# Attention over a long key cache on one core: K loaded in 8 KB rows and 1 MB transfers, V in 1 MB transfers, pairs of groups two apart

## The chip, the cores and the metric

The kernel runs on one core of one Trainium2 chip. The metric is the device time of one execution in microseconds (us), as the median of several runs. The profile of an execution has a span that is about 1.8 us shorter than that time. In the profile's lines PE is TensorE, DVE is VectorE, ACT is ScalarE, POOL is GpSimd and SP is SyncE. A DMA moves its bytes in packets; it has landed when its last semaphore update has come. A load here gives 16 such updates, as many as the profile counts DMA engines; below, each landing is read as that of one engine.

## The reference, cut to what matters

```python
B, Hq, Hkv, Sq, Sk, D = 16, 32, 8, 16, 2048, 128        # bf16 inputs
def reference(q, k, v):
    k = jnp.repeat(k, 4, axis=1); v = jnp.repeat(v, 4, axis=1)
    scores = jnp.einsum("bhqd,bhkd->bhqk", q, k) * D ** -0.5
    return jnp.einsum("bhqk,bhkd->bhqd", softmax(scores), v)
```

There are 16 x 8 = 128 groups. One group is one K and one V matrix of 2048 x 128 (512 KB each) and the 64 query rows (4 heads x 16) that share it. K and V are 134 MB together and every byte is used once. Q and the output are 2.1 MB each.

## The kernel before: the parts that the change and the argument touch

Two adjacent groups form a pair, so that 2 x 64 query rows fill 128 partitions. Each pair takes these steps: load K and V, transpose K on VectorE (one `eng.transpose` of 128 x 1024 32-bit words for each group, 1.24 us; the score matmuls then read it 32 partitions at a time), scores on TensorE, exp on ScalarE, transpose P on TensorE, copy it out of PSUM, P times V, scale by 1/rowsum, store. The order of instructions on each engine is fixed when the kernel is built, by a list scheduler in the kernel file. All DMAs are issued by SyncE, in one fixed order.

```python
# transfers, all on SP
if kind == "K":      # one group, 512 KB: 128 partitions x 4 KB
    dst, src = Kn[s].bitcast(BF16), kf[x].rearrange("(a j) d -> a (j d)", j=16)
elif kind == "V":    # one group, 512 KB: 128 partitions x 4 KB
    dst, src = Vb[s], vf[x].rearrange("(a j) d -> a j d", j=16)
...
else:                # ST: one pair, 32 KB: 128 partitions x 256 B
    dst, src = of[128 * x:128 * (x + 1), :], Osb[s]
sp.dma_start(dst, src).then_inc(prog.sem_dma[kind][s], 16)
...
# K transposed, then scores and exp over the 2048 keys of a pair
eng.transpose(KT[(p // 2) % NKT][:, p % 2, :], Kn[p % NBK])
eng.activation(P[p % 2]..., S_ps..., ACT.Exp, scale=scale, accum_out=rowsum[:, p:p+1])
...
# the end: exp without a maximum is safe only for sums within a range; if not, all is done again
eng.wait_ge(sem_flag, 4)
eng.reg_load(reg, flag)
eng.br_eq(reg, all_within, on_true=after, on_false=redo).branch_hint(hints[me])
```

Every engine ends with a branch over a large block of code (the second program, for the unsafe case). A hint for that branch (`branch_hint`) is placed some operations before the end (`HINT = {"pe": 7, "dve": 10, "act": 3, "pool": 1, "sp": 6}`).

## Time and profile before

| | before |
|---|---|
| time, median (runs) | 357.49 us (357.17 to 357.58) at first; 355.4 to 357.9 over all later runs |
| span of the profiled execution | 353.4 us |
| busiest compute engine | DVE, 68% of the span |
| packets of the kernel's DMA queue | 98.7% of 16 engines' span |

These lines of the profile's page of the kernel before give the span, the DMA share and rate in 40 slices of the span, the packets, the queues, and the kernel's DMAs with the median time from issue to landing.

```profile
span 353.4 us, 11937 instructions
...
DMA  7999999999999999999999999999999999999971
GB/s 276 414 408 408 413 408 407 412 413 406 413 408 410 412 410 412 408 413 411 410 411 411 408 412 413 395 411 413 409 411 409 406 413 410 403 409 405 411 287 42
DMA packets 47288, 139.24 MB, mean 394 GB/s; under 512 B 13440, under 2 KB 13440, under 8 KB 47232
...
q1 hardware_dynamic: 47232, 138.43, 98.7%
q8 instruction: 43, 0.70, 0.8%
...
Kn<-in_k_dram SPq DMA_DIRECT2D x128, 512.0 KB, 12.1
Vb<-in_v_dram SPq DMA_DIRECT2D x128, 512.0 KB, 13.3
...
out_dram<-O SPq DMA_DIRECT2D x64, 32.0 KB, 11.0
```

The reader should see a kernel that is bound by its DMA engines from slice 2 on: the DMA row stays at 9 up to slice 38, and no compute engine is busy for more than 68% of the span. By these figures only fewer bytes, cheaper packets or fewer packets can help inside the stream.

The trace's packet records give the price of a packet. The median is 159 ns for 4096 B, 84 ns for 2048 B, 18 ns for 256 B and 9 ns for a semaphore write of 4 B. A fit to these four is about 150 ns per 4 KB plus 9 ns per packet.

The second place to look is the end. These lines are the branch and the DRAIN that follows it on each engine (on SP, waits for the stores come between them, from 352.87 us on), from the queries for source lines 372 and 379; the columns are durations in ns and the start in us.

```profile
L372 ACTq COMPARE_BRANCH  x1: 72/72/72, 349.2 to 349.2; - x1
...
L372 SPq COMPARE_BRANCH  x1: 70/70/70, 349.6 to 349.6; - x1
...
L379 POOLq DRAIN  x1: 123/123/123, 349.7 to 349.7; - x1
L379 PEldq DRAIN  x1: 62/62/62, 349.8 to 349.8; - x1
L379 ACTq DRAIN  x1: 80/80/80, 352.6 to 352.6; - x1
L379 DVEq DRAIN  x1: 58/58/58, 352.7 to 352.7; - x1
L379 SPq DRAIN  x1: 7/7/7, 353.2 to 353.2; - x1
```

POOL and PE go on 0.5 us after the branch. ACT, DVE and SP stand still for 3.3 us, although the last store had landed at 350.10 us (the trace's semaphore landings). The chain of waits ends with the last scaling, at 348.28 + 0.35 = 348.63 us:

```profile
347.16 1.10 PE O_ps L355 x32
348.26 0.03 issue
348.28 0.35 DVE O L290
```

### The profile page before, as it was taken

The numbers are of one execution on the slowest core, as the hardware profiler recorded it, in microseconds if no ns is written. First come the engines' busy times: TensorE is split into PE (matmuls) and PEld (weight loads), VectorE is DVE, ScalarE is ACT, GpSimd is POOL, SyncE is SP. The second block draws the span as 40 slices with busy tenths as digits, with TensorE's granted clock in tenths as the row PEclk, the third lists the DMA queues.
The fourth block names the chain that finished last, engine by engine and source line by source line (L and its number), as shares of the span: only waits on it lengthen the run. The fifth ranks groups of instructions, "written<-read, shape, count | busy, mean of one in ns | idle before, by whom it ended". The sixth has DMA issues, their size and how long they took to land.

```text
span 353.4 us, 11937 instructions
## 1 busy us (share of the span) xinstructions
PE 233.8 (66%) x5378; PEld 167.9 (48%) x5378; DVE 239.4 (68%) x340; ACT 193.8 (55%) x214; POOL 28.9 (8%) x35
## 2 busy tenths in 40 slices
PE   2499765776666857756556876676656677566663
PEld 1266543554444634544444655454444545444442
DVE  4668786787685666766766676675776647866761
ACT  6458555754347646665456753576554755554450
POOL 1040000300012000310004000040000400000000
PEclk9999999989999998999999988999999989999997
DMA  7999999999999999999999999999999999999971
GB/s 276 414 408 408 413 408 407 412 413 406 413 408 410 412 410 412 408 413 411 410 411 411 408 412 413 395 411 413 409 411 409 406 413 410 403 409 405 411 287 42
DMA packets 47288, 139.24 MB, mean 394 GB/s; under 512 B 13440, under 2 KB 13440, under 8 KB 47232
## 3 DMA queue, kind: packets, MB, share of 16 engines
q1 hardware_dynamic: 47232, 138.43, 98.7%
q8 instruction: 43, 0.70, 0.8%
q14 instruction: 13, 0.11, 0.1%
HBM read 136.31 MB, written 2.10 MB: 392 GB/s over the span
## 4 chain that ended last, share of the span: by engine, by line
DMA 54%; PE 16%; DVE 14%; ACT 7%; SPq 5%; issue 4%
DMA Kn<-in_k_dram 54%; DVE KT L267 8%; ACT P L278 6%; PE S_ps L340 6%; SPq L317 5%; PE PT_ps L350 5%; PE O_ps L355 5%; DVE PT L299 4%; DVE O L290 1%; PE QT_ps L328 1%; ACT O L288 0%; DVE rrec L284 0%; DVE flag L419 0%
## 5 line engine op out<-in xcount | busy, mean ns | idle before, releaser
L267 DVE STREAM_TRANSPOSE KT<-Kn 128x1024 int32<-128x1024 int32 x128 | 158.1, 1238 | 75.7 <-DMA Kn<-in_k_dram 74.6
L278 ACT ACTIVATE P<-S_ps 128x2048 bf16<-128x2048 f32 x64 | 120.1, 1877 | 78.0 <-PE S_ps L340 77.8
L350 PE MATMUL PT_ps<-ident,P 128*128 128x128 bf16 x1024 | 76.0, 225 | 53.9 <-DVE PT L299 38.3
L340 PE MATMUL S_ps<-KT,QT 32*64 32x512 bf16 x2048 | 74.6, 398 | 45.8 <-DVE KT L267 16.8
L350 PEld LDWEIGHTS PT_ps<-ident,P 128*128 128x128 bf16 x1024 | 60.4, 100 | 77.8 <-issue 40.9
L299 DVE COPY PT<-PT_ps 128x1024 bf16<-128x1024 bf16 x102 | 66.1, 672 | 16.7 <-PE PT_ps L350 16.7
L355 PE MATMUL O_ps<-Vb,PT 128*64 128x128 bf16 x2048 | 73.1, 225 | 6.5 <-issue 5.4
L355 PEld LDWEIGHTS O_ps<-Vb,PT 128*64 128x64 bf16 x2048 | 61.8, 113 | 21.2 <-issue 16.9
L340 PEld LDWEIGHTS S_ps<-KT,QT 32*64 32x64 bf16 x2048 | 28.9, 105 | 69.0 <-DVE KT L267 34.3
L272 POOL COPY Qr<-Qn 128x1024 bf16<-128x1024 bf16 x28 | 27.9, 1041 | 250.4 <-DMA Qn<-in_q_dram 250.4
L288 ACT ACTIVATE O<-O_ps,rrec 128x128 bf16<-128x128 f32 x27 | 9.9, 367 | 56.7 <-PE O_ps L355 56.7
L299 ACT ACTIVATE QT<-QT_ps 128x1024 bf16<-128x1024 bf16 x30 | 30.6, 1019 | 6.6 <-PE QT_ps L328 6.6
L299 ACT ACTIVATE PT<-PT_ps 128x1024 bf16<-128x1024 bf16 x26 | 26.6, 1024 | 5.7 <-PE PT_ps L350 5.7
L328 PE MATMUL QT_ps<-ident,Qr 128*128 128x128 bf16 x256 | 22.4, 238 | 8.4 <-ACT Qr L272 4.5
L328 PEld LDWEIGHTS QT_ps<-ident,Qr 128*128 128x128 bf16 x256 | 17.4, 107 | 12.2 <-issue 7.4
L290 DVE TENSOR_SCALAR O<-O_ps,rrec 128x128 bf16<-128x128 f32 x37 | 12.7, 342 | 7.6 <-PE O_ps L355 7.2
L284 DVE RECIPROCAL rrec<-rowsum 128x1 f32<-128x1 f32 x64 | 9.5, 149 | 4.7 <-ACT P L278 3.8
L278 ACT ACTIVATION_READ_ACCUMULATOR P<-S_ps 128x1 f32 x64 | 12.4, 194 | 0.0
L272 DVE COPY Qr<-Qn 128x1024 bf16<-128x1024 bf16 x2 | 1.3, 690 | 3.3 <-DMA Qn<-in_q_dram 3.3
L299 DVE COPY QT<-QT_ps 128x1024 bf16<-128x1024 bf16 x2 | 2.5, 1225 | 1.2 <-PE QT_ps L328 1.1
L272 ACT ACTIVATE Qr<-Qn 128x1024 bf16<-128x1024 bf16 x2 | 2.0, 1049 | 1.3 <-DMA Qn<-in_q_dram 1.3
L272 ACT ACT_TABLE_LOAD x1 | 1.3, 1283 | 0.7 <-PEq L439 0.7
(12 smaller groups left out, 2.2 us busy)
## 6 DMA issues: line engine op xcount, KB each, us to landing
Kn<-in_k_dram SPq DMA_DIRECT2D x128, 512.0 KB, 12.1
Vb<-in_v_dram SPq DMA_DIRECT2D x128, 512.0 KB, 13.3
Qn<-in_q_dram SPq DMA_DIRECT2D x8, 256.0 KB, 12.0
out_dram<-O SPq DMA_DIRECT2D x64, 32.0 KB, 11.0
```

What stands on the lines that cost most here:

```text
L267: ins = eng.transpose(KT[(p // 2) % NKT][:, p % 2, :], Kn[p % NBK][:, :])
L272: ins = eng.activation(dst, src, ACT.Copy) if me == "act" else eng.tensor_copy(dst, src)
L278: ins = eng.activation(P[p % 2][:, :].rearrange("m (r a j) -> m a r j", a=4, j=32), src[:, :].rearrange("m (a r j) -> m a r j", a=4, j=32) ...
L284: ins = eng.reciprocal(rrec[:, p:p + 1], rowsum[:, p:p + 1])
L288: ins = eng.activation(dst, src, ACT.Copy, scale=r)
L290: ins = eng.tensor_scalar(dst, src, r, None, op0=ALU.mult)
L299: ins = eng.activation(dst, src, ACT.Copy) if me == "act" else eng.tensor_copy(dst, src)
L317: sp.dma_start(dst, src).then_inc(prog.sem_dma[kind][s], 16)
L328: ins = pe.transpose(QT_ps[:, 128 * i:128 * (i + 1)], Qr[:, x, i, :], ident[:, :],)
L340: ins = pe.matmul(S_ps[64 * gg:64 * (gg + 1), 512 * a:512 * (a + 1)], QT[c % 2][32 * a:32 * (a + 1), x, 128 * pp + 64 * gg:128 * pp + 64 * ...
L350: ins = pe.transpose(PT_ps[h][:, 128 * t:128 * (t + 1)], P[p % 2][:, 128 * r:128 * (r + 1)], ident[:, :])
L355: ins = pe.matmul(O_ps[64 * gg:64 * (gg + 1), 0:128], PT[p % NPT][:, r, 64 * gg:64 * (gg + 1)], Vb[(2 * p + gg) % NBV][:, r, :], start=(r ...
```

## The change

The intent is cheaper loading: K rows of 8 KB instead of 4 KB, and half as many load DMAs.

- One K load brings two adjacent groups. Each group fills 64 partitions with rows of 32 keys (8 KB).
- The keys of a partition are transposed in two halves, written interleaved (step of 8 bytes). A scores unit now covers half of the keys of two pairs, so exp runs on 1024 columns at a time and the two row sums are added.
- A pair is groups g and g+2, because the four groups of two K loads lie so in PSUM.
- V is loaded 1 MB at a time for a pair and lags K by five loads. The last V comes in two halves.
- Results of two pairs are stored together. Their rows do not form one regular pattern over 128 partitions, so there are two DMAs over 64 partitions each.
- The hints of the three engines that stood still for 3.3 us (ACT, DVE and SP) move far forward.

```diff
-NBK = 10
-NBV = 14
-NBO = 8
+NBK = 6
+NBV = 7
+NBO = 5
...
-HINT = {"pe": 7, "dve": 10, "act": 3, "pool": 1, "sp": 6}
+HINT = {"pe": 7, "dve": 200, "act": 10000, "pool": 1, "sp": 130}
...
+    def group_of(p, gg):
+        return 4 * (p // 2) + 2 * gg + p % 2
...
-                ins = eng.transpose(KT[(p // 2) % NKT][:, p % 2, :], Kn[p % NBK][:, :])
+                ins = eng.transpose(KT[p % NKT][:, gg, :, h],
+                                    Kn[(2 * p + gg) % prog.rings["K"]][:, J * 64 * h:J * 64 * (h + 1)])
...
-                dst, src = Kn[s][:, :].bitcast(BF16), kf[x].rearrange("(a j) d -> a (j d)", j=J)
-            elif kind == "V":
-                dst, src = Vb[s][:, :, :], vf[x].rearrange("(a j) d -> a j d", j=J)
+                dst = Kn[s][:, :].bitcast(BF16)
+                src = kf[2 * x:2 * x + 2].rearrange("g (b r) d -> (g b) (r d)", r=2 * J)
+            elif kind[0] == "V":
+                p, part = (x, slice(0, J)) if kind == "V" else (NP - 1, slice(J // 2 * x, J // 2 * (x + 1)))
+                g = group_of(p, 0)
+                dst = Vb[p % NBV][:, :, part, :].rearrange("a g r d -> a g (r d)")
+                src = vf[g:g + 3:2].rearrange("g (a r) d -> a g r d", r=J)[:, :, part, :].rearrange("a g r d -> a g (r d)")
...
-                dst, src = of[128 * x:128 * (x + 1), :], Osb[s][:, :]
+                for gg in range(2):
+                    g = 4 * x + 2 * gg
+                    sp.dma_start(of[64 * g:64 * (g + 2), :].rearrange("(p m) d -> m p d", p=2),
+                                 Osb[s][64 * gg:64 * (gg + 1), :, :]).then_inc(prog.sem_dma[kind][s], 16)
+                continue
```

## The prediction

> **What bounds the kernel now.** The DMA engines. No compute engine is busy above 68% of the 353.4 us span (DVE 68%, PE 66%, ACT 55%); the DMA part gives the packets of the kernel's own queue 98.7% of 16 engines' span, and the 40-slice row shows 403 to 416 GB/s from slice 2 on (one slice 395) until slice 39. The chain of waits is 54% "DMA Kn". The time is what the busiest DMA engines move, plus a tail.
>
> The DMA packet records give the sizes: 4096 B (32768 packets) median 159 ns, 2048 B 84 ns, 256 B 18 ns, the 4-byte semaphore write 9 ns. Those fit about 9 ns per packet plus 150 ns per 4 KB. Successive 512 KB loads land 1.275 to 1.28 us apart per engine, close to 8 x 159 + 9 ns. The 16 landings of one load spread from 1 us early to 7 to 8 us at the end: half of the engines are late, because 43 instruction fetches of 16 KB (1.08 us each) hit only those. The late half is busy until the last V lands at 347.0 us, so it sets the end.
>
> **What the change does.**
> 1. K rows 8 KB: 512 fewer packets per engine. An 8 KB packet should take about 309 ns (estimate from the fit) instead of 2 x 159: 512 x 9 ns = 4.6 us.
> 2. 127 fewer load DMAs: one 9 ns semaphore write per engine each, about 1.1 us.
> I take 5.0 us of these 5.7, nearly all on the critical path.
> 3. Compute: exp in halves. A 1024-column ACT copy takes 1.02 us and each accumulator read 0.19, so ACT grows by about 128 x 1.21 - 132 = 23 us (55 to about 61%); DVE gets 64 small adds of 0.15, +10 us. The chain scores, two exps, scores is about 1.1 + 2.4 + 0.3 = 3.8 us per 2 MB, against about 5.1 us of loading, so it hides. Transposes (1.24 us) and matmuls keep their counts, and I expect their durations (the score matmul still reads at a 4-byte step). The last V comes in halves: PE about 0.55 us shorter, but one more store issue, 0.35 us. Net -0.2.
> 4. Hints: at the end of the trace ACT, DVE and SP take the last branch at 349.2 to 349.6 and go on only at 352.6 to 352.9, while a 16 KB and several 8 KB instruction fetches run; PE and POOL go on at once. The change moves just those three hints far forward. If all three then hit, the end waits only for the last store (350.1): -2.7 us. I give it 0.65. [...]
>
> **Time.** 357.5 - 5.0 - 0.2 - 2.6 = 349.7 with the hints working, 352.3 without. Prediction 350.0 us, 347.5 to 353.0. Faster by over 2% 0.55, within 2% 0.43, slower 0.02.
>
> **What would show it.** 8192-byte packets x8192 at about 309 ns; 4096-byte ones at 159; loads at about 2.48 us (K) and 2.55 us (V) per engine; last V near 342; ACT, DVE and SP leaving the last branch within 0.3 us; transposes still 1.24 us.
>
> **What would make it wrong.** 8 KB rows split into 4 KB packets (gain falls to 1 us); strided transposes slowing DVE; the exp chain falling behind, with gaps in the DMA row; more instruction fetches on the late engines.

That the 43 instruction fetches hit only the late half of the engines was an inference when it was written; experiment 7 is what bears on it.

## The result

The changed kernel took 351.0 us (350.75 to 351.14, 4 runs) against 357.33 us (356.69 to 357.58, 4 runs). The ratio is 0.9825, with a 95% interval of 0.9808 to 0.9842. Ratios here are the mean time of one kernel's runs over that of the other's runs of the same rounds, so they are not quite the ratio of the medians quoted. The profiled execution of each run is left out of them. The kernel is 1.75% faster. The profiled execution of the kernel before was its fastest (355.28 us), so the two spans differ by 4.2 us only.

The same lines of the changed kernel's page:

```profile
span 349.2 us, 11953 instructions
...
DMA  7999999999999999999999999999999999999972
GB/s 310 425 411 414 414 409 413 416 412 413 413 417 411 416 415 409 413 415 415 414 414 414 412 414 415 412 417 415 411 416 411 414 417 414 417 412 411 388 292 55
DMA packets 37319, 139.23 MB, mean 399 GB/s; under 512 B 11408, under 2 KB 11408, under 8 KB 29072
...
q1 hardware_dynamic: 37264, 138.42, 98.2%
q8 instruction: 43, 0.70, 0.8%
...
Kn<-in_k_dram SPq DMA_DIRECT2D x64, 1024.0 KB, 17.0
Vb<-in_v_dram SPq DMA_DIRECT2D x63, 1024.0 KB, 17.3
...
out_dram<-O SPq DMA_DIRECT2D x64, 32.0 KB, 13.7
```

About 10,000 packets are gone. The rate inside the stream rose, but only from about 410 to 414 GB/s. The branch and the end of the chain of waits:

```profile
L417 ACTq COMPARE_BRANCH  x1: 72/72/72, 345.1 to 345.1; - x1
...
L417 SPq COMPARE_BRANCH  x1: 74/74/74, 346.7 to 346.7; - x1
...
L424 ACTq DRAIN  x1: 79/79/79, 345.6 to 345.6; - x1
...
L424 DVEq DRAIN  x1: 56/56/56, 345.8 to 345.8; - x1
L424 SPq DRAIN  x1: 7/7/7, 349.0 to 349.0; - x1
```

```profile
343.53 0.66 PE O_ps L400 x16
344.19 0.03 issue
344.21 0.35 DVE O L326
```

ACT and DVE no longer stall. Yet the span ends 4.7 us after the last scaling (344.56 to 349.2), nearly as late as before (348.63 to 353.4, 4.8 us). Split at the packets and semaphore landings of the two traces, the 4.2 us come from here:

| stretch, us | before | after | difference |
|---|---|---|---|
| start to the end of the last load packet | 346.60 | 343.04 | -3.56 |
| from there to the end of the last scaling | 2.03 | 1.52 | -0.51 |
| from there to the landing of the last store | 1.47 | 4.35 | +2.88 |
| from there to the end of the span | 3.30 | 0.31 | -2.99 |

The last two rows nearly cancel. That, and a first row smaller than the predicted 5.0, is what the experiments had to explain.

### The profile page after: what moved, and what is told of

Its sections match the earlier page's. It is cut to its first block, busy times and chain, and to the rows that moved or that the text cites. A ratio compares the mean times of both kernels' runs of the same rounds, so it can differ in the third digit from the quotient of the medians.

```text
span 349.2 us, 11953 instructions
## 1 busy us (share of the span) xinstructions
PE 240.3 (69%) x5378; PEld 171.6 (49%) x5378; DVE 220.9 (63%) x359; ACT 232.3 (67%) x387; POOL 28.9 (8%) x35
## 3 DMA queue, kind: packets, MB, share of 16 engines
q1 hardware_dynamic: 37264, 138.42, 98.2%
## 4 chain that ended last, share of the span: by engine, by line
DMA 68%; PE 13%; DVE 7%; ACT 7%; SPq 4%; issue 1%
DMA Kn<-in_k_dram 64%; PE S_ps L384 6%; DVE KT L293 6%; ACT P L312 4%; PE PT_ps L394 4%; DMA Vb<-in_v_dram 3%; SPq L358 3%; PE O_ps L400 2%; ACT PT L335 2%; SPq L361 1%; PE QT_ps L372 1%; ACT QT L335 1%; DVE PT L335 1%; DVE rowsum L318 0%; DVE rrec L320 0%
## 5 line engine op out<-in xcount | busy, mean ns | idle before, releaser
L312 ACT ACTIVATE P<-S_ps 128x1024 bf16<-128x1024 f32 x128 | 130.1, 1023 | 63.2 <-PE S_ps L384 53.9
L384 PE MATMUL S_ps<-KT,QT 32*64 32x512 bf16 x2048 | 78.2, 414 | 50.3 <-DVE KT L293 37.4
L335 ACT ACTIVATE PT<-PT_ps 128x1024 bf16<-128x1024 bf16 x60 | 61.3, 1021 | 4.2 <-PE PT_ps L394 4.1
L335 DVE COPY PT<-PT_ps 128x1024 bf16<-128x1024 bf16 x68 | 44.6, 662 | 1.8 <-PE PT_ps L394 1.6
L324 ACT ACTIVATE O<-O_ps,rrec 128x128 bf16<-128x128 f32 x44 | 16.1, 367 | 24.1 <-PE O_ps L400 24.1
L335 ACT ACTIVATE QT<-QT_ps 128x1024 bf16<-128x1024 bf16 x24 | 24.6, 1023 | 8.7 <-PE QT_ps L372 8.6
L312 ACT ACTIVATION_READ_ACCUMULATOR P<-S_ps 128x1 f32 x128 | 25.9, 203 | 0.0
L326 DVE TENSOR_SCALAR O<-O_ps,rrec 128x128 bf16<-128x128 f32 x20 | 6.6, 329 | 7.5 <-PE O_ps L400 7.4
L318 DVE TENSOR_TENSOR rowsum<-rhalf 128x1 f32<-128x1 f32 x64 | 9.5, 177 | 1.6 <-ACT P L312 1.6
L335 DVE COPY QT<-QT_ps 128x1024 bf16<-128x1024 bf16 x8 | 9.7, 1210 | 1.1 <-PE QT_ps L372 1.1
## 6 DMA issues: line engine op xcount, KB each, us to landing
Vb<-in_v_dram SPq DMA_DIRECT2D x63, 1024.0 KB, 17.3
```

The lines of the kernel that those rows point to most:

```text
L312: ins = eng.activation(P[p % 2][:, :].rearrange("m (r a h j) -> m h a r j", h=2, a=2, j=32)[:, h], src.rearrange("m (a r j) -> m a r j", a ...
L318: ins = eng.tensor_tensor(rowsum[:, p:p + 1], rhalf[:, p, 0:1], rhalf[:, p, 1:2], op=ALU.add)
L324: ins = eng.activation(dst, src, ACT.Copy, scale=r)
L335: ins = eng.activation(dst, src, ACT.Copy) if me == "act" else eng.tensor_copy(dst, src)
L384: ins = pe.matmul(S_ps[64 * gg:64 * (gg + 1), 512 * a:512 * (a + 1)], QT[c % 2][32 * a:32 * (a + 1), x, row:row + 64], kt[:, :, x // 2, p ...
```

## The experiments

Twelve kernels ran, each beside the kernel before on the same chip. The times of the kernel before in these rounds were 356.5 to 356.7 us (median), 0.6 to 0.8 us below those of the result's round. The changed kernel itself was not timed again; 351.0 us is from that first round. A difference to it of less than about 0.8 us therefore says little.

Two theories were set against each other. By theory A, the loads lost packet costs as counted, the stores in their new form gave part of it back, and the hint's gain vanished behind a last store that lands late. The rival B differed from run to run and is named in each expectation.

### 1. K rows as two 4 KB packets in the changed kernel

```diff
-    Kn = [sb(f"Kn{i}", [128, 2 * J * 64], I32) ...]
+    Kn = [sb(f"Kn{i}", [128, 2, J * 64 + 16], I32) ...]      # a gap of 64 B splits each row
-                dst = Kn[s][:, :].bitcast(BF16)
+                dst = Kn[s][:, :, 0:J * 64].bitcast(BF16)
```

> The changed kernel, but each 8 KB K row lands as two 4 KB packets (the K buffer has a gap of 64 bytes between its halves), still one 1 MB DMA. Theory A (the gain is the saved cost of 8192 packets): K loads take 2.55 us per engine again instead of 2.49, 64 x 0.066 us = 4.2 us longer: about 355.2 us against 351.0. Rival B (the per-packet cost is hidden once stores and V loads run, and the gain comes from fewer DMAs, deeper queues and the end): less than 2 us longer, below 353.

Measured: 353.81 us (353.27 to 354.65), ratio to before 0.9921 (0.9903 to 0.9939). The trace has 4096 B packets again, at a median of 159 ns, and as many more packets as the change had saved in its K rows:

```profile
DMA packets 45511, 139.23 MB, mean 395 GB/s; under 512 B 11408, under 2 KB 11408, under 8 KB 45456
```

So the 8 KB rows are worth 353.81 - 351.0 = 2.8 us (3.4 us by the two ratios to the kernel before). That is the largest part of the gain, but it is less than A's 4.2, and it lies between the two theories. In the trace, which is of this kernel's slowest execution, the last load packet ends at 346.31 us, against 343.04 in the changed kernel and 346.60 in the kernel before: in these traces 3.3 of the 3.56 us of the table's first row hang on the size of the K packets.

### 2. The old hints in the changed kernel, and the new hints in the kernel before

```diff
-HINT = {"pe": 7, "dve": 200, "act": 10000, "pool": 1, "sp": 130}
+HINT = {"pe": 7, "dve": 10, "act": 3, "pool": 1, "sp": 6}
```

> The changed kernel with the branch hints back at their old places (DVE 10, ACT 3, SP 6 operations before the end). Theory A: ACT, DVE and SP stall 3.3 us at the last branch again, but the last store of the changed kernel lands only 2.2 us after SP's branch, so most of the stall is hidden behind it: 0.8 to 2 us longer, about 352.3. Rival B (hints are worth the whole stall): 3 us longer, 354.

> The kernel before with only the three hints moved to the change's places. Theory A: the end waits for the last store alone, which lands at 350.1 us of the old span: about 2.7 us shorter, 354.7. Rival B (these places fit only the changed instruction streams): SP, ACT or DVE still stalls, no change, 357.3.

Measured: the changed kernel with the old hints took 351.0 us (350.85 to 351.15), the same as with the new ones. The kernel before with the new hints took 353.17 us (352.35 to 353.8), ratio 0.9908 (0.9888 to 0.9928), 3.4 us less than the kernel before beside it. So the hints are worth 3.4 us in the old kernel and nothing that can be seen in the changed one. For the kernel before, A (2.7 us) was near and B fell; for the changed kernel both were off, since even A had expected 0.8 to 2 us. In the kernel before with the new hints all three engines go on within 0.6 us of branches at 349.1 to 349.5 us, and the span ends 0.5 us after the last store's landing instead of 3.3:

```profile
L379 ACTq DRAIN  x1: 79/79/79, 349.6 to 349.6; - x1
...
L379 DVEq DRAIN  x1: 58/58/58, 349.8 to 349.8; - x1
L379 SPq DRAIN  x1: 7/7/7, 350.3 to 350.3; - x1
```

In the changed kernel with old hints, ACT goes on 3.4 us after its branch, but that is still before the last store has landed (348.95 us), which SP waits for:

```profile
L424 ACTq DRAIN  x1: 66/66/66, 348.6 to 348.6; - x1
L424 SPq DRAIN  x1: 7/7/7, 349.0 to 349.0; - x1
L424 DVEq DRAIN  x1: 40/40/40, 349.1 to 349.1; - x1
```

### 3. The new stores in the kernel before, in two forms

```diff
-                dst, src = of[128 * x:128 * (x + 1), :], Osb[s][:, :]
+                rows = of[256 * x:256 * (x + 1), :].rearrange("(p g m) d -> g m p d", p=2, g=2)
+                for gg in range(2):                      # half stores: two DMAs of 64 partitions
+                    sp.dma_start(rows[gg], Osb[s][64 * gg:64 * (gg + 1), :, :])...
```
```diff
+                dst, src = of[256 * x:256 * (x + 1), :].rearrange("(p q) d -> q p d", p=2), Osb[s]   # pair stores: one DMA
```

> The kernel before, only its stores as in the change: two pairs' results in one buffer, written by two DMAs of 64 partitions x 2 rows each instead of two DMAs of 128 partitions x 1 row. Theory A (the new stores hold up the DMA engines more: 0.069 us each against 0.03, from the spacing of the loads): 64 x 0.04 = 2.5 us longer before the end, plus up to 1 us at the end for the second issue: 359 to 361. Rival B (stores cost the stream the same in either form, the missing gain lies elsewhere): only the end moves, at most 1 us longer, 357.3 to 358.3.

> The kernel before with two pairs' results in one store over all 128 partitions (32 DMAs of 64 KB instead of 64 of 32 KB). Theory A (it is the 64-partition halves, two DMAs, that cost, not two rows per partition or the later store): within 0.7 us of the kernel before, and below the variant with half stores by 0.7 us or more; landing within 2 us of the last scaling. Rival B (two rows per partition or the pairing of stores costs): as slow as the variant with half stores, 1 us above the kernel before.

Measured: half stores took 357.49 us (ratio 1.0031, 1.0012 to 1.005), pair stores 357.3 us (ratio 1.0015, 0.9994 to 1.0037). Half stores thus fit B. Pair stores fit neither theory: A wanted them 0.7 us or more below half stores, B 1 us above the kernel before. In the stream both lost the same small amount (see the table in section 5), so the form of the store is not what costs the stream 2 us. That part of A falls. At the end they differ: from the last scaling to the landing it takes 4.37 us with half stores and 1.68 us with pair stores.

### 4. One store over all 128 partitions in the changed kernel, with new and with old hints

The two pairs' rows do form a regular pattern if each group's half of the result is scaled separately, into partitions chosen by the pair instead of the group. That costs 64 more small scalings.

```diff
-                dst, src, r = Osb[p // 2 % NBO][:, p % 2, :], O_ps[:, 0:128], rrec[:, p:p + 1]
+                to, fro = (slice(64 * x, 64 * (x + 1)) for x in (p % 2, op[2]))
+                dst, src, r = Osb[p // 2 % NBO][to, op[2], :], O_ps[fro, 0:128], rrec[fro, p:p + 1]
...
+                dst, src = of[256 * x:256 * (x + 1), :].rearrange("(g q) d -> q g d", g=2), Osb[s]
```

> The changed kernel, but each group's half of the result is scaled by itself into partitions 64 x (pair odd or even), so that two pairs' results go out in one DMA over 128 partitions (32 stores of 64 KB instead of 64 of 32 KB over 64 partitions). Theory A (the two half stores delay the end: 4.35 us from the last scaling to the landing, against 1.47 in the kernel before; and they cost the load stream about 2 us): the landing falls to about 1.5 us, 2.8 us shorter, and 1 to 2 us more from the stream: about 347. Rival B (the late landing comes from the hints, whose instruction fetches run at that moment, not from the stores' form): no shorter than 350.

> The changed kernel with full 128-partition stores (348.2 us) and the branch hints back at the old places. Theory A (a stall at the last branch and a late last store run side by side, and the later one counts): with the store landing 1.75 us after the last scaling, the 3.3 us stall of ACT and DVE is no longer hidden: 2 to 2.7 us longer, about 350.7, though with the half stores the same edit cost nothing. Rival B (the hints do nothing in the changed kernel): 348.2.

Measured: with full stores 348.21 us (348.11 to 348.4), ratio 0.9763 (0.9743 to 0.9783), correct. With full stores and old hints the runs took 351.31 to 352.17 us, ratio 0.9859 (0.9838 to 0.988); one more execution took 728.67 us and is left out; nothing on record explains it. The four kernels make a square:

| | old hints | new hints |
|---|---|---|
| half stores (as changed) | 351.0 | 351.0 |
| full stores | 351.6 | 348.2 |

Neither edit alone gains anything, and both together gain 2.8 us. A's other part, 1 to 2 us from the stream, did not come (348.2, where A said about 347). The stall at the branch and the late landing run side by side, and the later one counts. The lines that show it are the stores issued in the last microseconds, from the DMA view of 344 to 354 us with the count, the size and the median us to landing, first for the changed kernel, then for full stores:

```profile
out_dram<-O SPq DMA_DIRECT2D x2, 32.0 KB, 2.8
```

```profile
out_dram<-O SPq DMA_DIRECT2D x1, 64.0 KB, 1.6
```

The trace suggests why two stores land so much later than one. SP needs 0.60 us for each of the two issues, so the second leaves at 345.84 us, against one issue of 0.37 us. About 1 us after the branch of ACT and DVE, instruction fetches of 8 and 16 KB begin; the page counts their queues (q14 and q8) as shares of the same 16 DMA engines. In the changed kernel that is at 346.22 us, while the second store is on its way: 12 of its 16 completions land by 347.19 us and the other four at 348.51 to 348.91. With the full store all 16 have landed by 346.23 us, and the fetches begin at 346.26. The packets fit this: 16 of the 128 packets of 256 B of the second half store took 44 to 196 ns instead of 18, and its last ones began only at 347.6 us; none of the full store's took over 40 ns. That the four late completions wait behind the fetches is an inference from these times; no run moved the fetches alone.

And the branch with full stores and old hints, the price of the stall no longer hidden:

```profile
L422 ACTq DRAIN  x1: 81/81/81, 349.1 to 349.1; - x1
L422 SPq DRAIN  x1: 7/7/7, 349.5 to 349.5; - x1
```

### 5. Hardly any stores in either kernel (wrong results on purpose)

```diff
-        if p % 2:                                    # changed kernel; the kernel before likewise
+        if p == NP - 1:
             add(("ST", p // 2), ("nm", p - 1), ("nm", p))
```

> The changed kernel with only the last of its 32 pairs of stores (wrong result on purpose). Theory A (the packets saved on K and V are worth the full 4.9 us only where no stores run; stores cost the changed kernel's load stream about 0.55 us per 8 pairs): steady state 41.0 us per 8 pairs instead of 41.5, 4.4 us shorter: about 346.6. Rival B (stores cost 0.24 us per 8 pairs as in the kernel before): 2 us shorter, 349.

> The kernel before with only its last store (wrong result on purpose). Theory A: stores cost it 0.24 us per 8 pairs: steady state 41.55 us per 8 pairs instead of 41.80, 2 us shorter, about 354.7; against the changed kernel without stores the step per 8 pairs is then 0.6 us. Rival B (stores cost both kernels the same 4.4 us): 352.3.

Measured: the changed kernel without stores took 348.31 us (348.1 to 348.36), ratio 0.9764; the kernel before without stores 355.37 us (353.27 to 356.37), ratio 0.9953 (0.9922 to 0.9984). Both gained less than A said, because at the end other things took over: in the changed kernel the last load packet came 3.9 us earlier but the last scaling only 2.9, and in the kernel before the last scaling came 4.9 us after the last load packet instead of 2.0. The stream itself is clean of that. This table has the time that one DMA engine needs for the K, V, Q and results of eight pairs in the steady state: the earliest of the 16 landings of a pair's V load to that of the V load eight pairs later, median of five such stretches.

| us per 8 pairs | with stores | without |
|---|---|---|
| kernel before | 41.85 | 41.52 |
| changed kernel | 41.51 | 40.90 |
| changed, K in 4 KB packets | 41.72 | |
| changed, full stores | 41.48 | |
| before, half stores | 41.94 | |
| before, pair stores | 41.91 | |

Without stores the two kernels differ by 0.62 us, and 8 x 0.62 = 5.0 us, the gain that was predicted for the loads. With stores they differ by 0.34, and 8 x 0.34 = 2.7 us. The stores cost the changed kernel 0.61 us per eight pairs (0.58 as full stores) and the kernel before 0.33 (0.39 to 0.42 in the new forms). Another choice of the five stretches moves these figures by up to 0.07. Because the engines that come last set the end, they were checked too: a straight line through the mean of the eight late landings, pairs 8 to 56, gives 0.62 us between the two kernels without stores and 0.39 with them (42.53, 41.91, 42.86 and 42.47 us per eight pairs). Stretches from 60 to 300 us show the same in GB/s (last column; the DMA share before it stays above 1), for the kernel before, the changed kernel, and the two without stores in the same order:

```profile
60.00:300.00 240.00, 163.01 (x3784) 117.63 (x3785) 164.74 (x232) 135.30 (x151) 23.94 (x24) 0.96 1.03 410
```

```profile
60.00:300.00 240.00, 167.38 (x3819) 119.81 (x3816) 154.25 (x249) 165.32 (x281) 19.96 (x20) 0.94 1.03 414
```

```profile
60.00:300.00 240.00, 164.74 (x3806) 121.04 (x3806) 172.00 (x237) 131.33 (x149) 23.97 (x24) 0.96 1.03 407
```

```profile
60.00:300.00 240.00, 171.12 (x3804) 121.53 (x3800) 158.02 (x262) 162.60 (x262) 19.97 (x20) 0.90 1.02 413
```

The kernels without stores move 1.5% fewer bytes (137.2 against 139.2 MB), so by an estimate from these rates 410 against 407 means that the stores rode along half free, and 414 against 413 that they mostly did not.

### 6. V in 512 KB loads

```diff
+            if kind == "V":
+                for gg in range(2):
+                    sp.dma_start(dst[:, gg], src[:, gg]).then_inc(prog.sem_dma[kind][s], 16)
+                continue
```

> The changed kernel with each 1 MB V load issued as two 512 KB loads (packets as before, 63 DMAs more). Theory A (a DMA more costs an engine only its semaphore write, about 9 ns): 63 x 0.01 = 0.6 us longer or less, within 351.0 to 351.7. Rival B (larger loads are the gain, because a DMA costs much more than its semaphore write): 2 us longer, 353.

Measured: 351.15 us (350.63 to 352.23), ratio 0.9843 (0.9822 to 0.9863), the same as the changed kernel within the spread. Behind the queue of this kernel, in which a V load lands 17.3 us (median) after its issue, the size of a V load is worth nothing that can be seen; the 0.6 us that A allowed could hide in the spread, B's 2 us could not.

### 7. Fewer matmuls, so fewer instruction fetches (wrong results on purpose)

```diff
-                rs = range(J) if p < NP - 1 else range(J // 2 * op[2], J // 2 * (op[2] + 1))
+                rs = range(0, J, 2) if p < NP - 1 else range(J // 2 * op[2], J // 2 * (op[2] + 1), 2)
```

> The changed kernel with every second key block left out of P times V (wrong result on purpose): 1024 matmuls fewer, the loads, stores and waits unchanged. Theory A (each 16 KB instruction fetch takes 1.07 us of one of the 8 late DMA engines, and those engines set the end): 35 instead of 43 fetches, 8 x 1.07 / 8 = 1.1 us shorter, plus 0.3 us of a shorter last PV; about 349.6. Rival B (the fetches only use slack): at most the 0.3 us, 350.7.

Measured: 349.46 us (348.68 to 349.81), ratio 0.9795 (0.9773 to 0.9817): 1.5 us shorter than the changed kernel, where A said 1.4 and B 0.3. The intervals of the two ratios just overlap, so the trace has to decide. The instruction queue's line fell from 43 packets to 35:

```profile
q8 instruction: 35, 0.57, 0.7%
```

The last load packet ended at 341.68 us instead of 343.04. Only the late half of the DMA engines gained: per eight pairs, by the straight line of section 5, the eight late landings went from 42.47 to 42.27 us, and the eight early ones stayed (41.55 and 41.54). Had the shorter TensorE work freed buffers sooner, the early ones should have gained as well. So the instructions of this unrolled TensorE program cost the kernel time although PE is busy in only 69% of the span. The reading that fits these landings is that they are fetched over the DMA engines that bound it, and only by some of them (8 fetches fewer over 8 late engines would be 8 x 1.07 / 8 = 1.07 us by A's estimate): in the changed kernel eight of the 16 landings of the last V load come at 336.2 to 337.0 us and eight at 341.8 to 343.5.

### 8. Four of the eight Q loads in parts of 119 and 9 partitions

```diff
+                if x in (2, 3, 4, 5):
+                    sp.dma_start(dst[:119], src[:119]).then_inc(prog.sem_dma[kind][s], 16)
+                    sp.dma_start(dst[119:], src[119:]).then_inc(prog.sem_dma[kind][s], 16)
+                    continue
```

> The changed kernel with four of the eight Q loads split into 119 and 9 partitions[...]. Theory A1 [...]: 2 to 2.7 us shorter, about 348.5. Rival A2 [...]: about 3 us longer, 354. Rival B (a late half does not set the end): no change, 351.

The grounds of A1 and A2 are cut from this expectation: they rested on which DMA engines such a load uses, and no trace here shows that. What is left are estimates for the case that the late engines get less of Q's work (A1) or more of it (A2).

Measured: 359.89 us (358.67 to 361.14), ratio 1.0092 (1.0065 to 1.0119), longer than any of the three said (348.5, 354 and 351), and so no answer to which engines are late. The semaphores of these loads show 16 landings for the two parts together, as many as a whole Q load has in the changed kernel. While such Q loads ran, the DMA share stayed at 1.02 to 1.03 but the rate fell to 353 to 379 GB/s from 412 in a stretch without one, and 12 to 30% of the 4 KB packets of the other loads took over 220 ns, about 240 at their median, instead of 159. What they collide on was not tested. Which half of the DMA engines fetches the instructions stays open.

## Why the prediction was right or wrong

The predicted time was 350.0 us, with a range of 347.5 to 353.0. Measured were 351.0, inside the range. The prediction leaned slightly to faster by over 2% (0.55 against 0.43); measured were 1.75%, so the lean was to the wrong side of a close line.

- **What bounds the kernel: right.** The DMA row stays at 9 in both kernels, from slice 2 to slice 38 (98.7 and 98.2% of 16 engines' span for the kernel's own queue), and taking packets away shortened the time (353.81 against 351.0 us, experiment 1).
- **The price of a packet: right.** 8192 B packets took 309 ns (median), as estimated. In the changed kernel before its first store (at 35 us), K loads landed 2.49 us and V loads 2.55 us apart; 2.48 and 2.55 had been written. Transposes took 1.23 us, unchanged.
- **"I take 5.0 us of these 5.7, nearly all on the critical path": mis-sized.** The last load packet came 3.6 us earlier. The 5.0 us are there without stores (8 x 0.62), but with stores 2.7 us of them are left in the steady state (3.1 by the late engines), because stores cost the leaner stream 0.61 us per eight pairs instead of 0.33. The estimate came from a stretch with loads alone and was applied to a stretch with stores. The rest of the 3.6 comes about at the start: the first two of the 40 slices moved 310 and 425 GB/s instead of 276 and 414, which is worth about 1 us (an estimate from these slices). Why stores cost more there was not settled: of the 0.28 us that they cost more, the new form explains at most 0.09, the table's difference in the kernel before; that they filled gaps which the 4 KB packets left is a possible reading that no run tested.
- **127 fewer DMAs, 1.1 us: not seen in the V part.** 63 of those DMAs, added back, changed the time by 0.15 us, where 0.6 was counted, but single executions spread from 350.63 to 352.23 us (experiment 6).
- **The hints, "-2.7 us": the mechanism was right, the sum was wrong.** ACT and DVE went on 0.5 to 0.6 us after the branch, as hoped, and the hints alone save the kernel before 3.4 us. In the changed kernel they saved nothing. The prediction took the landing of the last store from the old trace ("the end waits only for the last store (350.1)") and counted for the new store only a second issue, "0.35 us". That step failed: the issues took 0.60 us each and the landing came 4.35 us after the last scaling instead of 1.47. Here the two effects, which end at the same barrier, did not add; the square in experiment 4 shows it (351.0, 351.0, 351.6 and 348.2 us). One store over all partitions was better at the end of the kernel than two over halves (landing after 1.75 against 4.35 us), and in the stream the two forms were the same (41.48 against 41.51 us), so that two were no gain anywhere.
- **Compute hides: right, though its numbers were off.** ACT was to grow by 23 us and grew by 38.5 (193.8 to 232.3), and DVE fell by 18.5 where +10 was written. The list scheduler gave ACT 60 of the P copies instead of 26. Neither bounds the kernel, and nothing on record shows that this cost time; no run tested it.

The missing size was thus made up of -3.6 for -5.0 in the stream and about -0.6 for -2.9 after it (the lower three rows of the result's table). The profiled executions differ by 4.2 us and the timed ones by 6.3; the time of the kernel before spreads over 2.5 us from run to run, and no run explains that spread. So there was luck in the number: the prediction took its terms from a trace of the fastest execution (355.28 us) and subtracted 7.8 us of them from the median of other executions (357.5). Against its own trace it was off by 3.6 us, of which the higher starting point gave back 2.2.

## What to carry to other kernels

At the end of a kernel, find out which of the waits that end at the last barrier comes last before counting the gain of removing one; here the saved stall was worth only its lead over the next wait (nothing beside half stores, 351.6 - 348.2 = 3.4 us beside full ones). A last store as one DMA over all partitions landed 2.6 us sooner here than as two halves; that it should be out before the instruction fetches begin is argued from the times, not tested. When packets are priced from a stretch of pure loads, check the price again where loads and stores mix (here a gain of 0.62 us per eight pairs became 0.34), best with a run that has no stores. The version that combines the new loads, the new hints and full stores took 348.2 us, 2.4% faster than the kernel before.
